# Attention beside a gated MLP on one core: the spatial stage in cycles of eight steps

## The chip, the core and the metric

The kernel runs on one core of a Trainium2 chip. The core has a matrix engine (TensorE, PE in the profile, with its weight loads shown as PEld), a vector engine (VectorE, DVE), an engine for functions of one value (ScalarE, ACT), a general engine (GpSimd, POOL) and one that issues transfers (SyncE, SP). Matrix products land in PSUM, of which the kernel uses eight banks of 128 partitions by 512 numbers; VectorE and ScalarE read them from there. The metric is the device time of one execution in microseconds (us); smaller is better.

## What is computed

One normalised input of 2048 rows and 512 columns feeds two branches, whose outputs are added to the input.

```python
xn = layernorm(x)                         # 2048 x 512
# A: attention, 32 heads of 16
q, k, v = split(xn @ wqkv)
p = softmax(q @ k.T * 16 ** -0.5)         # 32 x 2048 x 2048
a = (p @ v) @ wo
# B: gated MLP with a product over the rows
z = gelu(xn @ w_in)                       # 2048 x 1792
z1, z2 = z[:, :896], layernorm(z[:, 896:])
g = w_sp @ z2 + b_sp[:, None]             # w_sp: 2048 x 2048
b = (z1 * g) @ w_out
out = x + a + b
```

All is in 32-bit numbers. The "dense" products (all but attention's) are made in three parts, high by high, low by high and high by low, from operands split in a high and a low part.

## The kernel before

**Attention as 1024 steps.** Two heads share a pass: half 0 of TensorE's rows holds one, half 1 the other. There are 16 pairs of heads, 4 blocks of 512 queries each and 16 blocks of 128 keys each, so 16 x 4 x 16 = 1024 steps. A step makes, for each of its two heads,

- the scores of 128 keys against 512 queries (`score`, tile `st`, L1274) and their exponentials on ScalarE (L1277, tile `pf`, a buffer of two halves, `PF` = 6 buffers);
- the maxima that a later step needs (`max_one`, tile `mx`, L904): the scores the other way round, and a reduction on VectorE (L905). They run `LEAD` = 26 steps ahead; every 16 steps `max_fin` gathers them and sends them through memory into rows of Q;
- the V products (`pv`, tile `o`, L1232): the exponentials against V and a column of ones, for four column tiles of TensorE at once, added up in one bank over 16 steps.

Scores, maxima and dense products are "lanes": they use 64 rows of TensorE, and two lanes, one on each half, run at the same time. I call two such lanes a pair. The V products use all 128 rows in tiles of 32 columns.

**Cycles.** The loop at the end of `fused_block` goes on by `steps` steps at a time, four of them (`STEPS`). A cycle is: `gather` takes dense products from the front of `queue`; `share` says how many of them go into this cycle; `fill` orders the scores of these steps, the maxima and the dense products on the two halves; `pv_some` issues V products up to step `b + steps - 2`, so they lag by two steps; then the copies of finished accumulators and the gathering of maxima. Every bank of scores or maxima is one of five (`rsum`, tags r0 to r4): a product that comes sixth waits until ScalarE or VectorE has emptied one. Two more banks (d0, d1) hold dense sums, one holds `o`.

**Order.** `fill` plans with its own numbers for time (`SLOT`, `ROUND`, `EXP`, `RED`): it tries greedy orders, then `better` moves products about. `length` and `rollout` price an order by its end and by how far the work left on ScalarE and VectorE goes beyond it (`TURN`).

**Dense work.** `queue` holds six generators: `qk_first`, `z2_all`, `z1_all`, `spatial`, `mlp_out` (mo), `attn_out` (ao). `halves` makes two sums at a time; each half of TensorE adds to one sum, and at each number in `cuts` the halves change sums, with a break in `gather` (`SWAP`). In `spatial` a group is two blocks of 128 columns of z2 against one block of 512 rows of `w_sp`: 16 cells of 3 products, 48 slots, twice, so 192 lanes; each fourth group of a block of rows has one block of columns (`whole`, 96 lanes). Its operands are 16 pieces of weights (`wsp`, split by GpSimd in `prepare`) and pieces of z2 (`zs`, fetched by `load_z`), all from a ring of `RING` = 25 pieces of 4 KB a partition. `pace` and `credit` spread what dense work is left over what steps are left.

Of the kernel before, what the change touches and what calls it, by code (L numbers as in the profile page):

```python
# [33 lines left out]
GC = 0.7978845608028654  # L34
RING = 25
WARM = 15
LEAD = 26
PF = 6
SWAP, END, GATE = 1.25, 1.5, 1.75
STEPS = 4  # L40
# [9 lines left out]
CAP = 3.3  # L50
FIRST = 6
BIAS = 0.0, 0.15, 0.3, 0.6


@with_exitstack
def fused_block(ctx, tc, x, wqkv, wo, w_in, w_spT, b_sp, w_out, out):
# [74 lines left out]
    def slow(us, fn, *args):  # L131
        later(us, waiting.append, (fn, args))
# [10 lines left out]
    def clock():  # L143
        return max(lanes)
# [28 lines left out]
    def later(us, fn, *args):  # L173
        late.append((clock() + us, len(late), fn, args))
# [540 lines left out]


    def spatial():
        zp, z1s, hls = {}, {}, {}
# [25 lines left out]
        for n, (g, fs) in enumerate(groups):  # L744
# [39 lines left out]
            cells = [(lambda s=s: part(s)) for s in range(NT)]  # L784
            want = STEPS * pace + credit / 4
            cuts = (12, 24, 36) if want > 11.4 else (12, 20, 36) if want > 10.2 else (12, 20, 32)
            if single:
# [10 lines left out]
            else:  # L798
                yield from halves(accs, cells, cuts, done)
                for u, f in enumerate(fs):  # L800
# [324 lines left out]
    with tc.manual_schedule(engines=engines):  # L1125
# [90 lines left out]
        maxed = []  # L1216
        lastS = [0, 0]

        def pv(n, a, w):
# [111 lines left out]
        def rollout(ns, want, start, most, bias, extra, flip, rng):  # L1331
# [57 lines left out]
            end_ = max(l)  # L1389
            cost = end_ + 0.3 * sum(max(0.0, v - end_ - TURN) for v in load_) - GAIN * more  # L1390
            return cost, ops

        def length(ops, want, start):
# [29 lines left out]
            end_ = max(l0, l1)  # L1423
            return end_ + 0.3 * (max(0.0, va - end_ - TURN) + max(0.0, vd - end_ - TURN))

# [95 lines left out]
        while b < N or done < N:  # L1521
            steps = 1 if b < 0 else STEPS if b else 2
            ns = [n for n in range(b, b + steps) if 0 <= n < N]
            ms = [m for m in range(b + LEAD, b + LEAD + steps) if m < NSTEP]
            for n in range(b, b + steps):
# [4 lines left out]
                if n > 16 and n % 16 == 2 and n // 16 + 3 < NG * NP:  # L1530
                    load_q(n // 16 + 3)
            pause = max(0, pause - steps)
# [5 lines left out]
            gather(FIRST if b < 0 else 0)  # L1538
            fill(ns, ms, len(slots) if b < 0 else share())
# [3 lines left out]
            if b >= 0:  # L1543
                pv_some(min(b + steps - 2, N))
            nds = []
# [79 lines left out]
```

## Time and profile before

| what | value |
|---|---|
| median of 2 runs | 1791.36 us (1790.3 and 1792.41) |
| the profiled execution | 1790.37 us, its span 1788.3 us |
| granted TensorE clock, mean | 0.999 |
| matmul records | 14419 |
| from the first product of the spatial stage's first cycle | 600.85 us into the span |
| of the first mo cycle | 1467.72 us |
| of the first ao cycle | 1672.52 us |

The span is cut into places by time from its start. A row of the timeline has the start, the length, the engine, the line, the operation, output and inputs by the program's names, the shape, and how many such instructions were merged. A row of the table by stretches has the stretch, its length, and the busy time of PE, PEld, DVE, ACT and POOL with instruction counts, then the granted clock, the share of DMA time and GB/s. The rows themselves stand in the prediction, where they are used. The eight V products that a cycle of four steps issues are 16 records in the trace, four a step.

### The profile page before, as it was taken

How to read it: one execution, taken by the hardware profiler on the slowest of the kernel's cores; microseconds unless marked ns; L12 is line 12 of the kernel's file. 1: busy time of each engine (PE TensorE's matmuls, PEld its weight loads, DVE VectorE, ACT ScalarE, POOL GpSimd, SP SyncE). 2: the span in 40 equal slices, each digit the busy share in tenths (PEclk: the TensorE clock that was granted, in tenths of full speed). 3: DMA queues.
4: the chain of work that ended last, by engine and by line, in shares of the span. 5: the costliest groups of instructions: out<-in, count | busy, mean ns of one | idle time of the engine just before them, and what ended most of it. 6: DMA issues, size and time to landing. Idle time of an engine off the chain costs nothing.

```text
span 1788.3 us, 37962 instructions
## 1 busy us (share of the span) xinstructions
PE 1777.3 (99%) x14419; PEld 1140.7 (64%) x14419; DVE 1449.6 (81%) x2604; ACT 1267.0 (71%) x2351; POOL 782.5 (44%) x815
## 2 busy tenths in 40 slices
PE   9999999999999999999999999999999999999998
PEld 7876666666666666666666566666666666666664
DVE  5288888988888888888888888888877888888872
ACT  5338788887777777777777777777776777677765
POOL 4257676777412542257334573224765261003220
PEclk9999999999999999999999999999999999999999
DMA  7552443534645744356445564345766454454534
GB/s 282 201 171 78 133 127 104 170 88 125 198 150 172 221 140 116 109 171 183 133 144 176 173 195 115 105 126 164 200 180 179 142 169 134 149 170 150 160 108 135
DMA packets 218254, 274.63 MB, mean 154 GB/s; under 512 B 35752, under 2 KB 119352, under 8 KB 216632
## 3 DMA queue, kind: packets, MB, share of 16 engines
q1 hardware_dynamic: 215336, 263.47, 49.1%
q0 software_dynamic: 2592, 8.46, 1.2%
q8 instruction: 114, 1.87, 0.5%
q14 instruction: 68, 0.56, 0.1%
q10 hardware_dynamic: 144, 0.26, 0.0%
HBM read 178.55 MB, written 93.58 MB: 152 GB/s over the span
## 4 chain that ended last, share of the span: by engine, by line
PE 96%; DMA 1%; DVE 1%; ACT 1%; SPq 0%; issue 0%; POOL 0%; DVEq 0%; POOLq 0%; ACTq 0%
PE o L1232 26%; PE st L1274 18%; PE sp L233 17%; PE mx L904 13%; PE z2p L233 5%; PE mo L233 4%; PE z1p L233 3%; PE qk L233 3%; PE ao L233 2%; PE duo L233 2%; PE v L221 1%; PE v L222 1%; PE v L223 1%; DMA zs<-z2scr 0%; PE qk L221 0%; PE qk L222 0%
## 5 line engine op out<-in xcount | busy, mean ns | idle before, releaser
L905 DVE TENSOR_REDUCE mm<-mx 128x1 f32<-128x512 f32 x2048 | 1291.2, 685 | 249.4 <-PE mx L904 214.6
L1277 ACT ACTIVATE pf<-st 128x512 f32<-128x512 f32 x2048 | 1102.9, 601 | 361.9 <-PE mx L904 211.1
L1274 PE MATMUL st<-qst,kst 50*128 50x512 f32 x2048 | 764.4, 410 | 0.8 <-ACT pf L1277 0.7
L904 PE MATMUL mx<-kst,qst 48*128 48x512 f32 x2048 | 752.3, 412 | 0.1
L1274 PEld LDWEIGHTS st<-qst,kst 50*128 50x128 f32 x2048 | 361.0, 185 | 248.1 <-issue 116.8
L233 PE MATMUL sp<-wsp,zs 64*128 64x512 f32 x2688 | 510.2, 393 | 0.0
L1232 PE MATMUL o<-pf,vall 128*32 128x512 f32 x4096 | 492.5, 598 | 0.0
L904 PEld LDWEIGHTS mx<-kst,qst 48*128 48x128 f32 x2048 | 361.8, 185 | 63.4 <-ACT pf L1277 11.6
L233 PEld LDWEIGHTS sp<-wsp,zs 64*128 64x128 f32 x2688 | 366.2, 186 | 29.9
L1232 PEld LDWEIGHTS o<-pf,vall 128*32 128x32 f32 x4096 | 107.0, 109 | 235.2 <-issue 215.7
L233 PE MATMUL mo<-wout,hp 64*128 64x512 f32 x672 | 124.5, 392 | 0.0
L233 PEld LDWEIGHTS mo<-wout,hp 64*128 64x128 f32 x672 | 90.5, 186 | 9.6
L539 POOL TENSOR_TENSOR hhl<-z1i 128x512 f32<-128x512 f32 x28 | 29.2, 1042 | 148.0 <-DMA z1i<-z1scr 118.4
L78 ACT ACTIVATE e<-o 128x512 f32<-128x512 f32 x64 | 38.4, 599 | 70.0 <-PE o L1232 65.8
L861 POOL TENSOR_TENSOR xr<-mox,xr 128x512 f32<-128x512 f32 x8 | 10.3, 1285 | 131.3 <-ACT mox L78 131.3
L545 POOL TENSOR_SCALAR hhl<-hhl 128x512 f32<-128x512 f32 x28 | 17.4, 621 | 104.0 <-ACT hhl L78 104.0
L967 POOL TENSOR_TENSOR ob<-ob 128x512 f32<-128x512 f32 (+1 forms) x16 | 20.7, 1292 | 96.3 <-DMA ob<-rscr 96.3
L805 POOL TENSOR_TENSOR hhl<-hhl,brow 128x512 f32<-128x512 f32 x12 | 15.4, 1287 | 83.5 <-ACT hhl L78 80.7
L233 PE MATMUL ao<-wo,op 64*128 64x512 f32 x288 | 51.9, 392 | 0.0
L586 POOL TENSOR_TENSOR z<-z,z2u 128x896 fp32r<-128x896 f32 x16 | 34.1, 2130 | 27.4 <-ACT z2u L78 27.4
L1039 POOL TENSOR_TENSOR fin<-aox,fin 128x512 f32<-128x512 f32 x8 | 10.3, 1282 | 74.9 <-ACT aox L78 74.9
L233 PEld LDWEIGHTS ao<-wo,op 64*128 64x128 f32 x288 | 36.4, 186 | 4.1
(293 smaller groups left out, 1955.6 us busy)
## 6 DMA issues: line engine op xcount, KB each, us to landing
zs<-z2scr SPq DMA_DIRECT2D x112, 512.0 KB
escr<-e SPq DMA_DIRECT2D x60, 256.0 KB
hscr<-hhl SPq DMA_DIRECT2D x28, 512.0 KB
xscr<-xnT POOLq DMA_DIRECT2D x16, 512.0 KB, 4.9
qscr<-qkhl SPq DMA_DIRECT2D x16, 512.0 KB
kscr<-qkhl SPq DMA_DIRECT2D x16, 512.0 KB
qst<-qscr SPq DMA_DIRECT2D x128, 64.0 KB
hp<-hscr SPq DMA_DIRECT2D x16, 512.0 KB
```

Of the source, the lines that this page charges most:

```text
L78: return nc.scalar.activation(out, in_, func, **kw)
L221: nc.tensor.matmul(acc, lh, rh, start=first, stop=False)
L222: nc.tensor.matmul(acc, ll, rh, start=False, stop=False)
L233: made[half] = lambda: nc.tensor.matmul(acc, prod[0][rows], prod[1][rows], start=start, stop=stop)
L539: gps(0.0022 * n).tensor_mul(u, x, x)
L586: gps(2.1).tensor_sub(low, z, u)
L904: nc.tensor.matmul(acc, qst[c][rows, t * P:(t + 1) * P], kst[p % 2][rows, kc * 512:(kc + 1) * 512], start=True, stop=True)
L905: nc.vector.tensor_reduce(mmax[i // 16][:, j, t, kc:kc + 1], acc, AX.X, ALU.max)
L967: gps(1.3).tensor_mul(both[rows, 0, :], both[rows, 0, :], both[rows, 2, :])
L1232: nc.tensor.matmul(acc[cols:cols + VW, a:a + w], vpack(kt - 1 + r, 2 * p + j), pf[:, j * 512 + a:j * 512 + a + w], start=kt == 1 and a == ...
L1274: nc.tensor.matmul(st, kst[p % 2][rows, kt * P:(kt + 1) * P], qst[c][rows, :], start=True, stop=True)
L1277: nc.scalar.activation(full[n][:, j * 512:(j + 1) * 512], st, AF.Exp, scale=0.25)
```

## The change

The exponentials get eight buffers, the ring 23 pieces: 8 KB a partition move from one to the other. While the spatial stage runs (the list `wide` is not empty), a cycle has eight steps if its first step is a multiple of eight and at least 20 dense slots are gathered, and takes up to 24 of them in one batch; otherwise four steps. `cuts` become (24, 24), so that a batch ends where the halves change sums. In a cycle that ends at a multiple of four, V products are issued up to its last step, with no lag. `gather` now runs before the steps are counted. A piece of z counts as there 4 us after its issue, and one of the second half up to 4 us before that. `slack` replaces `TURN`, for ScalarE and VectorE apart, by the length of the V products to come. Once two generators are left in `queue`, the pace aims at an end of mo at step 926 (`BEGIN`), and a batch may be cut in parts of six slots instead of eight.

```diff
-RING = 25
+RING = 23
-PF = 6
+PF = 8
+BEGIN = 926
...
+                if end_ and f == 6:
+                    wide.append(True)
...
-            later(4.0, zp.update, {(g, f, i): t})
+            zp[g, f, i], due[g, f, i] = t, clock() + 4.0
...
-                if (g, s) not in wsp or any((g, f, s // 4) not in zp for f in fs):
+                if (g, s) not in wsp or any(due.get((g, f, s // 4), 1e9) > clock() + s // 4 % 2 * 4.0 for f in fs):
...
-            want = STEPS * pace + credit / 4
-            cuts = (12, 24, 36) if want > 11.4 else (12, 20, 36) if want > 10.2 else (12, 20, 32)
+            cuts = (24, 24)
...
+        wide.clear()
...
-            cost = end_ + 0.3 * sum(max(0.0, v - end_ - TURN) for v in load_) - GAIN * more
+            cost = end_ + 0.3 * sum(max(0.0, v - end_ - s_) for v, s_ in zip(load_, slack)) - GAIN * more
...
-            n = max(round(r / max(aim + credit / 4, 3)), math.ceil(r / (CAP * STEPS)), 1)
-            n = min(n, max(r // 8, 1))
+            if wide:
+                return 8 if steps == 4 and b % 8 and r >= 20 else math.ceil(r / max(math.ceil(r / (3.4 * steps)), 1))
+            n = max(round(r / max(aim + credit / 4, 3)), math.ceil(r / (CAP * steps)), 1)
+            n = min(n, max(r // (6 if len(queue) < 3 else 8), 1))
...
+            if b > 0:
+                pause = max(0, pause - turned)
+                gather(0)
+                if wide:
+                    if b % 8 == 2:
+                        steps = 6
+                    elif b % 8 == 0 and len(slots) >= 20:
+                        steps = 8
+                elif b % 4 == 0:
+                    steps = 6
+            turned = steps
+            held = 2 if b < 0 or (b + steps) % 4 else 0
+            gone_ = 0.43 * (min(b + steps - held, N) - done) + 0.34
+            slack[:] = gone_ - (0 if held else 0.95), gone_
...
+                if len(queue) == 2:
+                    pace = max((todo - 192) / max(BEGIN - b, 4), 0)
...
-                pv_some(min(b + steps - 2, N))
+                pv_some(min(b + steps - held, N))
```

What this makes of the order is seen on TensorE. First, the end of a cycle in the spatial stage, before. The names are those of the lists above (`st` scores, `mx` maxima, `sp` dense products of this stage, `o` V products from one buffer of exponentials each, `x2` for two rows alike); brackets name the engines or queues whose semaphore a row waits for.

```order
L233 MATMUL sp_2_1_9683<-wsp_3_8390,zs_3_0_9334 128x512
L904 MATMUL mx_1_9849<-kst_90,qst_87 128x512 [waits Activation_49]
L1274 MATMUL st_0_9852<-qst_85,kst_90 128x512 [waits DVE_49]
L1232 MATMUL o_0_9659<-pf_9719,vall 32x512 x2
L1232 MATMUL o_0_9659<-pf_9741,vall 32x512 x2
L1232 MATMUL o_0_9659<-pf_9784,vall 32x512 x2
L1232 MATMUL o_0_9659<-pf_9801,vall 32x512 x2
L1274 MATMUL st_0_9865<-qst_85,kst_90 128x512 [waits Activation_49]
```

The same place after:

```order
L234 MATMUL sp_2_1_9716<-wsp_7_8748,zs_3_1_9682 128x512
L1280 MATMUL st_0_9885<-qst_85,kst_90 128x512 [waits DVE_49]
L1238 MATMUL o_0_9684<-pf_9720,vall 32x512 x2
L1238 MATMUL o_0_9684<-pf_9739,vall 32x512 x2
L1238 MATMUL o_0_9684<-pf_9770,vall 32x512 x2
L1238 MATMUL o_0_9684<-pf_9785,vall 32x512 x2
L1238 MATMUL o_0_9684<-pf_9807,vall 32x512 x2
L1238 MATMUL o_0_9684<-pf_9812,vall 32x512 x2
L1238 MATMUL o_0_9684<-pf_9823,vall 32x512 x2
L1238 MATMUL o_0_9684<-pf_9839,vall 32x512 [waits Activation_49]
L1238 MATMUL o_0_9684<-pf_9839,vall 32x512
L1280 MATMUL st_0_9908<-qst_86,kst_90 128x512 [waits DMAHW2_49]
```

Four buffers of exponentials were used up in one group of V products, and now eight are, the last of them filled in the same cycle, with a wait for ScalarE.

Second, TensorE in the mo stage, before: the end of a cycle that has 24 dense products (`mo`).

```order
L233 MATMUL mo_1_22195<-wout_21147,hp_0_21829 128x512
L904 MATMUL mx_0_22263<-kst_90,qst_88 128x512 [waits DVE_49]
L233 MATMUL mo_1_22195<-wout_21249,hp_0_21829 128x512
L904 MATMUL mx_0_22267<-kst_90,qst_88 128x512 [waits Activation_49]
L233 MATMUL mo_1_22195<-wout_21249,hp_0_21829 128x512
L233 MATMUL mo_0_22194<-wout_21249,hp_0_21827 128x512
L233 MATMUL mo_1_22195<-wout_21249,hp_0_21829 128x512
L1274 MATMUL st_0_22273<-qst_87,kst_90 128x512 [waits DVE_49]
```

After, the end of one that has 12:

```order
L234 MATMUL mo_0_21308<-wout_20444,hp_0_20778 128x512 x2
L234 MATMUL mo_1_21309<-wout_20444,hp_0_20780 128x512 x2
L1280 MATMUL st_0_21364<-qst_88,kst_89 128x512 [waits Activation_49]
L909 MATMUL mx_1_21369<-kst_90,qst_85 128x512 [waits DVE_49]
L909 MATMUL mx_0_21372<-kst_90,qst_85 128x512 [waits Activation_49]
L909 MATMUL mx_1_21375<-kst_90,qst_85 128x512 [waits DVE_49]
L1280 MATMUL st_0_21378<-qst_88,kst_89 128x512 [waits Activation_49]
```

Scores and maxima, each waiting for a bank that another engine empties, now stand together with no dense product between them. In counts: the spatial stage had 137 cycles of four steps and has 45 of eight and 36 of four; mo had 32 cycles of 18 to 24 dense products and has 41, of which 21 have 14 or fewer. Scores, maxima, exponentials, V products and dense products are as many as before.

More of the change, by code (lines that the diff above doesn't have):

```diff
@@ L714, in sp_weights @@
         return f"wsp{g}_{s}", w_spT[s * P:(s + 1) * P, g * 512:(g + 1) * 512], 512
+    wide = []
     def spatial():
-        zp, z1s, hls = {}, {}, {}
+        zp, due, z1s, hls = {}, {}, {}, {}
         def load_z(g, f, i):
@@ L1217, in fused_block @@
         lastS = [0, 0]
+        slack = [TURN, TURN]
         def pv(n, a, w):
@@ L1423, in length @@
             end_ = max(l0, l1)
-            return end_ + 0.3 * (max(0.0, va - end_ - TURN) + max(0.0, vd - end_ - TURN))
+            return end_ + 0.3 * (max(0.0, va - end_ - slack[0]) + max(0.0, vd - end_ - slack[1]))
         def better(cost, ops, want, start, rng, n):
@@ L1531, in fused_block @@
                     load_q(n // 16 + 3)
-            pause = max(0, pause - steps)
+            if b <= 0:
+                pause = max(0, pause - steps)
             if b >= 0:
@@ L1535, in fused_block @@
                 pace = (todo - spare) / max(N - 4 - b, 4)
+                if len(queue) == 2:
+                    pace = max((todo - 192) / max(BEGIN - b, 4), 0)
                 aim = steps * max(pace + 0.5 * (not ms), 0)
                 credit = min(credit + aim, 4 * steps)
-            gather(FIRST if b < 0 else 0)
+            if b <= 0:
+                gather(FIRST if b < 0 else 0)
             fill(ns, ms, len(slots) if b < 0 else share())
```

## The prediction

> **What bounds the kernel now.** I read the page's busy shares and its chain first.
>
> ```profile
> PE 1777.3 (99%) x14419; PEld 1140.7 (64%) x14419; DVE 1449.6 (81%) x2604; ACT 1267.0 (71%) x2351; POOL 782.5 (44%) x815
> ...
> PE 96%; DMA 1%; DVE 1%; ACT 1%; SPq 0%; issue 0%; POOL 0%; DVEq 0%; POOLq 0%; ACTq 0%
> ```
>
> TensorE is never seen idle, and 96% of the chain is its own. But ends of matmuls are modelled, so a full row does not say that every microsecond is needed. What a cycle is worth must be read from its length. I therefore looked at the timeline of TensorE in the stretch where a cycle with 24 dense products (twelve pairs) is followed by one with only 6. A cycle here runs from the first score to the next first score after the V products.
>
> ```profile
> 1304.86 0.50 PE L1274 MATMUL st<-qst,kst 50*128 50x512 f32 x1
> ...
> 1305.66 0.86 PE L233 MATMUL sp<-wsp,zs 64*128 64x512 f32 x6
> ...
> 1309.38 0.39 PE L1274 MATMUL st<-qst,kst 50*128 50x512 f32 x1
> 1309.70 1.92 PE L1232 MATMUL o<-pf,vall 128*32 128x512 f32 x16
> 1311.56 0.50 PE L1274 MATMUL st<-qst,kst 50*128 50x512 f32 x1
> ...
> 1315.78 1.92 PE L1232 MATMUL o<-pf,vall 128*32 128x512 f32 x16
> 1317.64 0.50 PE L1274 MATMUL st<-qst,kst 50*128 50x512 f32 x1
> ```
>
> The full cycle takes 1311.56 - 1304.86 = 6.70 us. The nearly empty one takes 1317.64 - 1311.56 = 6.08 us, though it has nine pairs of products less. So there are two limits. The timelines of VectorE and ScalarE in the same stretch name the second.
>
> ```profile
> 1312.12 4.97 DVE L905 TENSOR_REDUCE mm<-mx 128x1 f32<-128x512 f32 x8 [1.66 <-PE mx L904]
> ...
> 1309.84 0.60 ACT L1277 ACTIVATE pf<-st 128x512 f32<-128x512 f32 x1 [0.32 <-PE st L1274]
> ...
> 1312.24 4.25 ACT L1277 ACTIVATE pf<-st 128x512 f32<-128x512 f32 x8
> ```
>
> In the nearly empty cycle the eight maxima run without a gap for 4.97 us and the eight exponentials for 4.25 us. Sixteen scores and maxima pass through five PSUM banks, and TensorE must wait for a bank. Those three fences are the kernel in small: **a cycle is paid by TensorE if it has enough dense products, and by the emptying of the five banks if it has not.**
>
> The second limit also holds in a run, not only once. The table by stretches gives the spatial stage, the stage of the last product of the gated branch (mo), and eight cycles in a row with 16 dense products.
>
> ```profile
> 600.85:1467.72 866.87, 866.77 (x7076) 539.72 (x7073) 726.19 (x1291) 625.91 (x1173) 399.67 (x408) 1.00 0.53 155
> 1467.72:1672.52 204.80, 204.80 (x1700) 128.26 (x1696) 173.51 (x307) 145.85 (x273) 36.99 (x40) 1.00 0.49 152
> 1001.53:1050.39 48.86, 48.86 (x388) 28.60 (x384) 42.15 (x76) 36.79 (x70) 30.74 (x32) 1.00 0.57 171
> ```
>
> 48.86 / 8 = 6.11 us for a cycle of sixteen pairs (eight of scores and maxima, eight dense). The granted clock is 1.00 in all three, so it is no term of the sum.
>
> **Prices.** The six dense products at 1305.66 are three pairs in 0.86 us, and a lone pair lasts 0.39 in these rows, so a pair costs (0.86 - 0.39) / 2 = 0.235 us. The V products of one step are four records; the weight loads show their spacing.
>
> ```profile
> 1037.02 0.13 PEld L1232 LDWEIGHTS o<-pf,vall 128*32 128x32 f32 x4 [0.30 <-issue]
> 1037.45 0.13 PEld L1232 LDWEIGHTS o<-pf,vall 128*32 128x32 f32 x4 [0.30 <-issue]
> ```
>
> That is 0.43 us a step. A full cycle of four steps has 20 pairs, so what is left over, the entry to and the exit from the V products, is 6.70 - 20 x 0.235 - 4 x 0.43 = 0.28 us; with 0.23 for a pair it is 0.38. I take 0.33. This is what a cycle of double length pays once instead of twice: 2 x 6.70 - 0.33 = 13.07, which I take as 13.08 us.
>
> Five cycles with 20 dense products, and one block of four mo cycles with 24, 22, 20 and 18:
>
> ```profile
> 895.07 0.50 PE L1274 MATMUL st<-qst,kst 50*128 50x512 f32 x1
> ...
> 926.53 0.50 PE L1274 MATMUL st<-qst,kst 50*128 50x512 f32 x1
> ...
> 1467.72 0.50 PE L1274 MATMUL st<-qst,kst 50*128 50x512 f32 x1
> ...
> 1493.28 0.50 PE L1274 MATMUL st<-qst,kst 50*128 50x512 f32 x1
> ```
>
> 31.46 / 5 = 6.29 us, and 25.56 us for the block, which leaves 12.57 for 22 and 18 together: 6.47 and 6.10. From 18 downward I price every cycle at 6.11, the mean of the run above, next to the 6.08 of the cycle with 6.
>
> **The change, part by part.** The built order of TensorE gives the counts; the rows above give the prices.
>
> *Spatial stage.* Before: 137 cycles, 548 steps, 866.9 us. After: 45 cycles of eight steps with 48 dense products, 34 of four steps with 18 or fewer (they stand where the 16 weight pieces of the next group are brought in), two with 24; 504 steps. 45 x 13.08 + 34 x 6.11 + 2 x 6.70 = 588.6 + 207.7 + 13.4 = 809.7 us, which is -57.2.
>
> *Stage mo.* The 44 steps that the spatial stage no longer uses do not vanish: the scores, maxima and exponentials are still 1024 steps. The pace aims at step 926 for the start of the next stage, so the same 672 products of mo spread over 166 steps instead of 128. After: one cycle of six steps, 25 cycles of four with 6 to 18 dense products, and fifteen with 18 to 24. The six-step cycle has 24 scores and maxima in place of 16: the emptying part, 6.08 - 1.86 = 4.22 (from 1311.56 to 1315.78), grows to 6.3, and with the V products it is 8.2. 8.2 + 25 x 6.11 + 4 x (6.47 + 6.29 + 6.10) + 3 x 6.70 = 256.5 us against 204.8: +51.7. **Here the gain is given back**: cycles which had up to 24 dense products, and were paid by TensorE, get 12 to 14 and are paid by the banks.
>
> *Ends.* The last cycle of the z1 stage has six steps, takes V products of eight, and has 24 pairs: 24 x 0.235 + 8 x 0.43 + 0.33 = 9.4 for 6.70, +2.7. The end of the program has one full cycle more (+6.70), while the last one, which was filled with 24 dense products, keeps only four scores:
>
> ```profile
> 1772.85 0.73 PE L1274 MATMUL st<-qst,kst 50*128 50x512 f32 x3
> ...
> 1776.29 1.92 PE L1232 MATMUL o<-pf,vall 128*32 128x512 f32 x16
> 1778.14 1.12 PE L1063 MATMUL al<-fin,ident 128*128 128x512 f32 x2
> ```
>
> It took 5.29 us. Bare, it must wait for its four exponentials: 0.68 until the first begins (1311.56 to 1312.24), 2.2 for four, then the second half of the V products, 0.97: 3.9. So +6.70 - 1.4 = +5.3.
>
> *Wait for the own exponentials.* In the spatial stage the V products no longer lag by two steps. The last exponential of the full cycle ends at 1309.84 + 0.60 = 1310.44, 0.74 after the V products begin. In a cycle of four steps its V products come 0.86 after the beginning, in a doubled one 2.58. I take nothing; the cover is the earlier V products, and without it each exponential left over costs 4.25 / 8 = 0.53. Below zero it cannot go: a wait removed here was not seen.
>
> *Buffers.* Eight buffers of exponentials instead of six remove no wait, since none of the eight exponentials above waits between its neighbours. The ring of 23 must hold 16 weight pieces and 6 of z, one spare. Loads of z then stand behind a read of TensorE more often (66 of 112 in the built order, 24 before):
>
> ```profile
> SPq L123 <- PE sp L233: 65.1, 24, 11.1
> ```
>
> Behind such a load stand SP's other transfers: rows of maxima, K, Q. Nothing of TensorE waited for them; a piece is now fetched half a doubled cycle (6.5 us) before its use. I take nothing; if that cover goes, a late piece stalls TensorE by its own lateness. The slack numbers, the due times of z and the limit on a batch's parts change only the order, priced above.
>
> **Sum.** -57.2 + 51.7 + 2.7 + 5.3 = +2.5 us on the profiled execution of 1790.4 (span 1788.3, and 2.1 around it), so 1792.9; the median of the runs, 1791.4, is 1.0 above it. I write 1793.
>
> The Trainium skill, page "TensorEngine Tiling (Array Packing)", section "PSUM Bottleneck", warns that packing speeds up TensorE but not the emptying of PSUM, which may become the limit. That speaks against this change, for it saves TensorE's time alone. The trace agrees (6.08 us for the nearly empty cycle). With the rule the sum is 1793; without it, with every cycle priced by pairs, it would be the first rival's 1757.
>
> **Rivals.**
> 1. *The floor gives way*, and sparse cycles cost only their pairs (2.0 + 0.235 a pair: 5.76 with 16 dense products, 5.53 with 14, 5.29 with 12, 4.59 with 6). That takes 19 us off the spatial stage and 17 off mo: 1757. For it: VectorE is busy for 42.15 of the 48.86 us, so it is not full itself. Against: 6.08 and 48.86 / 8.
> 2. *Slower: the V products wait for exponentials of their own cycle.* With two left over when the V products begin, each of the 34 short cycles pays 0.74 + 0.53 - 0.86 = 0.41: +14, 1807. It turns into a slowdown of 2% (36 us more) if the doubled cycles too wait 0.45, which needs four to five exponentials left at their end: 34 x 0.45 + 45 x 0.45 = 36, so 1829. Against: the order puts one score at the end of the doubled cycle.
> 3. *Doubling saves nothing*: the left-over 0.33 goes with the number of V rounds and not with the entry. 45 x 0.32 = +14: 1807. Against: the spacing of 0.43 is even within a group.
> 4. *Late pieces of z or of weights*, one microsecond at each of some 16 groups: +16, 1809. The DMA share in the spatial stage, 0.53, leaves room.
>
> **How the numbers follow.** Chances: my sum 0.70, the rivals 0.05, 0.12, 0.07, 0.06. The sum's own bounds: a doubled cycle from 13.02 to 13.40 (-3, +14), a sparse cycle from 5.98 (the shortest, 1044.41 to 1050.39, below) to 6.31 in the 34 of the spatial stage (-8, +7).
>
> ```profile
> 1044.41 0.50 PE L1274 MATMUL st<-qst,kst 50*128 50x512 f32 x1
> ...
> 1050.39 0.50 PE L1274 MATMUL st<-qst,kst 50*128 50x512 f32 x1
> ```
>
> So 1782 to 1804 for my case, and 1780 to 1812 with rivals 3, 4 and the milder form of 2. Two per cent, 1755 to 1827, is about what a measurement of this kernel can tell from no change: faster 0.02 (the far end of rival 1), same 0.95, slower 0.03 (the full form of rival 2).
>
> **What would show it.** Right: some 81 groups of V products in the spatial stage, doubled cycles near 13.1, the stage near 810 us, mo near 256 with cycles of 6.1 whatever their dense products. Wrong: sparse cycles near 5.5 (rival 1), weight loads of the V products that wait for an exponential (2), doubled cycles at 13.4 (3), TensorE behind a DMA of z (4).

## The result, and the profile after

The changed kernel takes 1805.80 us (two runs, 1803.64 and 1807.95) against 1791.36 us before: a ratio of 1.0083, with a 95% interval of 1.0067 to 1.0099. It is slower by 0.8%, which is less than the two per cent that the chances went by. The forecast was 1793, with a range of 1780 to 1812.

The page's busy shares and chain of waits after:

```profile
PE 1784.3 (99%) x14419; PEld 1167.2 (65%) x14419; DVE 1450.8 (81%) x2604; ACT 1250.6 (69%) x2351; POOL 781.0 (43%) x815
...
PE 96%; DMA 1%; DVE 1%; ACT 1%; POOL 0%; issue 0%; SPq 0%; DVEq 0%; ACTq 0%; POOLq 0%
```

Nothing in these two lines tells that the kernel is another one. TensorE is "99% busy" in both, and the chain is 96% its own in both. The table by stretches tells more. It has the spatial stage, mo, and ao with its last V products (length, busy time of PE, PEld, DVE, ACT and POOL with their records, granted clock, DMA share, GB/s):

```profile
609.98:1421.03 811.05, 810.79 (x6724) 533.84 (x6720) 674.26 (x1192) 564.94 (x1084) 393.06 (x402) 1.00 0.54 161
1421.03:1681.11 260.08, 256.93 (x1997) 153.30 (x1993) 219.66 (x392) 185.40 (x350) 39.55 (x44) 0.99 0.43 128
1681.11:1791.52 110.41, 110.41 (x944) 67.65 (x940) 68.69 (x123) 76.61 (x145) 22.88 (x22) 1.00 0.43 133
```

With the cycles counted in the timeline of TensorE (from the first score after one group of V products to the first score after the next), both profiled executions come apart into these stages. The span grew by 13.5 us, from 1788.3 to 1801.8.

| stage | before, us | after, us | forecast | measured |
|---|---|---|---|---|
| prologue, to the end of the first V products | 134.8 | 140.5 | 0 | +5.75 |
| z2, Q and K | 302.8 | 302.8 | 0 | 0 |
| z1 | 161.7 | 165.1 | +2.7 | +3.4 |
| spatial stage | 866.9 | 811.05 | -57.2 | -55.8 |
| mo | 204.8 | 260.1 | +51.7 | +55.3 |
| ao, to the last V products | 105.6 | 110.4 | +5.3 | +4.8 |
| rest | | | 0 | +0.1 |

The spatial stage did what it was to do. These are two of its doubled cycles in the timeline of TensorE:

```profile
646.77 0.50 PE L1280 MATMUL st<-qst,kst 50*128 50x512 f32 x1
...
656.26 3.64 PE L1238 MATMUL o<-pf,vall 128*32 128x512 f32 x32
659.83 0.50 PE L1280 MATMUL st<-qst,kst 50*128 50x512 f32 x1
...
669.38 3.64 PE L1238 MATMUL o<-pf,vall 128*32 128x512 f32 x32
672.95 0.49 PE L1280 MATMUL st<-qst,kst 50*128 50x512 f32 x1
```

659.83 - 646.77 = 13.06 and 672.95 - 659.83 = 13.12 us; the 45 of them lie between 13.06 and 13.25, mean 13.10. The V products of eight steps take 3.57 us in each, twice the 1.86 of four steps less 0.15. Sparse cycles, a little earlier, with 16 and 14 dense products:

```profile
616.24 0.50 PE L1280 MATMUL st<-qst,kst 50*128 50x512 f32 x1
...
622.36 0.50 PE L1280 MATMUL st<-qst,kst 50*128 50x512 f32 x1
...
628.41 0.49 PE L1280 MATMUL st<-qst,kst 50*128 50x512 f32 x1
```

6.12 and 6.05 us. In mo the 21 cycles with 14 or fewer take 6.05 us on average.

What the forecast lacked happened in the prologue. There TensorE multiplies Q, K and z1 (`duo`), and in the rows GpSimd (POOL) splits weight pieces into high and low parts (`w`), and takes the low parts of Q and K (`qkhl`):

```profile
106.14 0.56 POOL L328 CAST w<-w_1r 128x448 fp32r<-128x448 f32 x1 [12.66 <-PE duo L234]
...
107.88 3.80 POOL L493 TENSOR_TENSOR qkhl<-duo,qkhl 128x512 fp32r<-128x512 f32 x3
...
114.25 0.63 ACT L79 ACTIVATE qkhl<-duo 128x512 fp32r<-128x512 f32 x1 [13.56 <-DMA qscr<-qkhl]
...
115.42 1.91 PE L234 MATMUL duo<-xnT,wqk 64*128 64x512 f32 x9 [3.42 <-ACT duo L79]
```

Read from the top: GpSimd stood 12.66 us before a weight piece, because TensorE still read the block of the ring into which it was to go. The three low parts of Q and K stood behind it in GpSimd's queue. Their stores were late, so ScalarE waited 13.56 us for a store of Q, and TensorE 3.42 us for ScalarE. The table by stretches over that place shows a second cost behind the first:

```profile
108.00:110.00 2.00, 2.00 (x20) 1.49 (x18) 1.41 (x3) 0.00 (x0) 2.00 (x2) 1.00 0.00 0
...
112.00:114.00 2.00, 0.00 (x0) 0.00 (x0) 1.44 (x4) 0.00 (x0) 0.00 (x0) 1.00 1.03 381
...
117.00:119.00 2.00, 2.00 (x12) 1.52 (x12) 0.75 (x2) 0.00 (x0) 0.00 (x0) 0.50 0.81 300
119.00:121.00 2.00, 2.00 (x16) 1.59 (x14) 0.72 (x2) 0.00 (x0) 0.00 (x0) 0.72 1.03 292
```

```profile
116.00:122.00 6.00, 6.00 (x40) 4.76 (x40) 2.48 (x4) 0.85 (x2) 0.22 (x1) 0.72 0.77 251
```

After the idle time the granted clock fell to 0.50. TensorE is shown as busy all the time there, but with 12 products in 2 us where it had 20 before the wait. In the kernel before, ScalarE waited 0.7 us for a store of Q, and the same place has neither the gap nor the slow clock:

```profile
112.00:116.00 4.00, 3.90 (x34) 3.12 (x32) 3.30 (x6) 0.29 (x1) 1.84 (x3) 1.00 0.77 215
116.00:122.00 6.00, 6.00 (x54) 4.55 (x52) 4.59 (x8) 0.58 (x2) 3.31 (x4) 1.00 0.48 132
```

An idle time with a slow clock behind it stands at the start of mo too, in the cycle of six steps, timeline first:

```profile
1421.04 0.49 PE L1280 MATMUL st<-qst,kst 50*128 50x512 f32 x1
...
1423.29 0.46 PE L234 MATMUL mo<-wout,hp 64*128 64x512 f32 x1 [1.51 <-POOL wout L329]
...
1432.14 0.50 PE L1280 MATMUL st<-qst,kst 50*128 50x512 f32 x1
```

```profile
1421.00:1423.30 2.30, 0.79 (x9) 0.34 (x5) 0.69 (x1) 1.08 (x2) 2.22 (x4) 1.00 1.00 371
1423.30:1427.30 4.00, 4.00 (x21) 3.81 (x23) 2.67 (x4) 2.11 (x4) 3.76 (x5) 0.59 0.77 267
```

TensorE waited 1.51 us for GpSimd's split of a `wout` piece, and then ran 4 us at a mean clock of 0.59. The cycle took 1432.14 - 1421.04 = 11.10 us.

### The profile page after: what moved, and what is told of

Its sections match the earlier page's. It is cut to its first block, busy times and chain, and to the rows that moved or that the text cites. A ratio compares the mean times of both kernels' runs of the same rounds, so it can differ in the third digit from the quotient of the medians.

```text
span 1801.8 us, 38004 instructions
## 1 busy us (share of the span) xinstructions
PE 1784.3 (99%) x14419; PEld 1167.2 (65%) x14419; DVE 1450.8 (81%) x2604; ACT 1250.6 (69%) x2351; POOL 781.0 (43%) x815
## 4 chain that ended last, share of the span: by engine, by line
PE 96%; DMA 1%; DVE 1%; ACT 1%; POOL 0%; issue 0%; SPq 0%; DVEq 0%; ACTq 0%; POOLq 0%
PE o L1238 26%; PE sp L234 18%; PE st L1280 17%; PE mx L909 12%; PE z2p L234 5%; PE mo L234 5%; PE z1p L234 4%; PE qk L234 3%; PE ao L234 2%; PE duo L234 2%; PE v L222 1%; PE v L223 1%; PE v L224 1%; DMA z1scr<-z 0%; DVE mm L910 0%; PE qk L222 0%
## 5 line engine op out<-in xcount | busy, mean ns | idle before, releaser
L1283 ACT ACTIVATE pf<-st 128x512 f32<-128x512 f32 x2048 | 1086.8, 604 | 334.8 <-PE mx L909 182.2
L1238 PE MATMUL o<-pf,vall 128*32 128x512 f32 x4096 | 485.9, 597 | 0.0
L1238 PEld LDWEIGHTS o<-pf,vall 128*32 128x32 f32 x4096 | 115.0, 109 | 247.6 <-issue 216.4
L234 PE MATMUL mo<-wout,hp 64*128 64x512 f32 x672 | 138.9, 401 | 1.5 <-POOL wout L329 1.5
L866 POOL TENSOR_TENSOR xr<-mox,xr 128x512 f32<-128x512 f32 x8 | 10.3, 1285 | 182.6 <-ACT mox L79 178.8
L963 POOL TENSOR_TENSOR os<-os 128x32 f32<-128x32 f32 (+1 forms) x16 | 4.0, 251 | 83.0 <-DMA os<-escr 59.0
```

The costliest lines, as they stand in the source:

```text
L234: made[half] = lambda: nc.tensor.matmul(acc, prod[0][rows], prod[1][rows], start=start, stop=stop)
L1238: nc.tensor.matmul(acc[cols:cols + VW, a:a + w], vpack(kt - 1 + r, 2 * p + j), pf[:, j * 512 + a:j * 512 + a + w], start=kt == 1 and a == ...
L1283: nc.scalar.activation(full[n][:, j * 512:(j + 1) * 512], st, AF.Exp, scale=0.25)
```

## Experiments

Three theories were to be told apart. The first: the smaller ring costs the prologue, by the queue of GpSimd. The second: the doubled cycle saves TensorE 0.33 us, and this is given back because a cycle has a floor, set by the emptying of the PSUM banks, which more cycles now reach. The rival to both: the doubling saves nothing, or the loss comes from the new pacing. Ratios are to the kernel before, run on the same chip.

| kernel | us | ratio (95% interval) |
|---|---|---|
| before with a ring of 23 | 1794.06 | 1.0022 (1.0014 to 1.0031) |
| before with ring 23 and eight buffers | 1795.77 | 1.0032 (1.0020 to 1.0045) |
| the same, three blocks counted as free | 1789.53 | 0.9996 (0.9987 to 1.0005) |
| changed, three blocks counted as free | 1800.93 | 1.0054 (1.0042 to 1.0067) |
| changed, no doubled cycles | 1811.86 | 1.0114 (1.0098 to 1.0129) |
| changed, doubled cycles with 40 dense products | 1811.58 | 1.0115 (1.0101 to 1.0128) |
| the same, three blocks counted as free | 1806.47 | 1.0093 (1.0076 to 1.0110) |
| changed, no pace for mo | 1812.90 | 1.0122 (1.0107 to 1.0137) |
| changed, half of each maximum | 1797.72 | 1.0041 (1.0028 to 1.0054) |
| changed, half of each exponential | 1797.63 | 1.0040 (1.0026 to 1.0054) |
| changed, both halved | 1773.77 | 0.9909 (0.9892 to 0.9926) |
| before, both halved | 1767.88 | 0.9876 (0.9861 to 0.9891) |

### The ring alone

```diff
-RING = 25
+RING = 23
```

> The kernel before with the ring of 23 blocks in place of 25, and nothing else; its cycles stay what they were. Theory A (the smaller ring alone delays the prologue, because a weight piece then waits for a block that TensorE still reads, and GpSimd's split of Q and K stands behind that piece): the first V products come about 5.7 us later, ScalarE's split of Q and K waits some 13 us for a store, and the time is about 1797 us, +5.8. Rival B (the delay in the prologue comes from the new cycles or the eight buffers of exponentials): the prologue is unchanged and the time is 1791 us. Rival C (the ring also starves the spatial stage of pieces of z): 1805 us, with TensorE behind transfers of z there.

It became 1794.06 us, 0.22% above the kernel before, between A and B. Where the time went is as A said. The waits up to 150 us (what waited, for what, us in total, times, the longest) have the same pair, and the later stages are as before:

```profile
ACT qkhl L78 <- DMA qscr<-qkhl: 12.3, 1, 12.3
POOL w L327 <- PE duo L233: 12.1, 1, 12.1
```

```profile
604.35:1471.02 866.67, 866.33 (x7076) 536.77 (x7072) 725.78 (x1291) 625.79 (x1173) 398.43 (x407) 1.00 0.52 155
1471.02:1675.67 204.65, 204.65 (x1700) 127.86 (x1696) 173.41 (x307) 145.86 (x273) 36.93 (x40) 1.00 0.48 152
```

The first V products end 4.1 us later than before (138.84 for 134.78 in the table's sense). TensorE's wait for ScalarE is 2.2 us here, and the clock behind it (0.87 over the 4 us from 112, 0.80 over the next 6) costs 4 x 0.13 + 6 x 0.20 = 1.7 us more, which together are 3.9. C falls: the ring starves nothing in the spatial stage, 866.67 for 866.87.

### Ring and buffers without the new cycles

```diff
-RING = 25
+RING = 23
-PF = 6
+PF = 8
```

> The kernel before with the ring of 23 and with eight buffers of exponentials, and nothing else; its cycles hold what they held. The ring alone cost 3.9 us, all of it in the prologue, where the changed kernel loses some 6. Theory A (the two buffer numbers make up the whole loss of the prologue): 1796 to 1798 us, with the first V products 6 us later than before and later stages unchanged. Rival B (eight buffers neither cost nor gain, and the other 2 us of the prologue come from the rest of the change): 1794 to 1795 us. Rival C (eight buffers remove waits in the later stages): below 1793 us.

1795.77 us, and 4.7 us more in the prologue of the profile (139.45); spatial stage and mo are as before (867.4 and 204.7). By the time, +0.32% or 5.5 us (3.6 to 8.1 by its interval), A and B cannot be told apart with certainty; A is nearer. C falls: eight buffers remove no wait that mattered.

```diff
-        freed = [clock()] * 4
+        freed = [clock()] * 3
```

This line stands in the prologue (`qk_first`). It says how many blocks of the ring the planner may count as free for weights of z2 at that moment. Added to the kernel above:

> The same kernel, with three blocks of the ring counted as free in the prologue in place of four (24 dense products of the z2 stage move from the prologue into a cycle of their own). Theory A (GpSimd's wait for a block of the ring, ahead of its part of Q and K, is the whole cost of the smaller ring): ScalarE's wait for the store of Q goes and the time is 1790 to 1793 us, that of the kernel before. Rival B (the smaller ring costs in another way, or the moved products cost as much as the wait): 1794 to 1798 us.

A holds, half a microsecond below its range: 1789.53 us, 0.9996 of before. The waits and the clock of this kernel:

```profile
POOL w L327 <- PE duo L233: 3.0, 1, 3.0
ACT qkhl L78 <- DMA qscr<-qkhl: 0.7, 1, 0.7
```

```profile
112.00:116.00 4.00, 3.89 (x34) 3.11 (x32) 3.28 (x6) 0.55 (x2) 2.36 (x4) 1.00 0.80 223
116.00:122.00 6.00, 6.00 (x55) 4.54 (x54) 4.55 (x8) 0.26 (x1) 2.93 (x4) 1.00 0.36 115
```

ScalarE's wait fell from 12.2 us to 0.7, TensorE has 34 and 55 products at a clock of 1.00 where the changed kernel's rows had a long gap and a slow clock, and the first V products end 4.1 us earlier than without this line (135.4 for 139.45). So the smaller ring need not bring the wait: a count of four free blocks, which did no such harm with 25, let GpSimd come to a piece too early. That the wait is the whole price is not shown. The line also changes the plan behind it: z2, Q and K take 309.8 us for 302.8, and the spatial stage has 135 cycles for 137 and takes 854.7 us for 867.4. The count of three with a ring of 25 was not run, so a part of the 0.36% may belong to this other plan.

### The same line in the changed kernel

> The changed kernel, in which the prologue counts three blocks of the ring as free for weights of the z2 stage in place of four, so that GpSimd does not come to a piece whose block TensorE still reads. Theory A (GpSimd's wait in the prologue is what costs the 5.75 us there): ScalarE's wait of 13.6 us for a store of Q goes, the first V products come some 5 us earlier, and the time is about 1800 us. Rival B (the wait hides behind other work and the delay comes from something else): 1806 us with the first V products as late as in the changed kernel.

1800.93 us, A by its time. This and the run before it agree on what the line is worth: 1.0083 - 1.0054 = 0.29%, and 1.0032 - 0.9996 = 0.36%, 5 to 6.5 us, each give or take some 3 us by the intervals. The 0.54% that are left, 9.7 us, belong to the rest of the change. In the profile the spatial stage has 809.7 and mo 258.1 us, about what the changed kernel has. ScalarE's long wait is gone there, but the first V products end 3.0 us earlier (137.6 for 140.5) and not 5: the granted clock was 0.74 over the 20 us from 130, which is 5.2 us lost. The moved products make z2, Q and K longer by 7.7 us and z1 shorter by 4.1, so mo begins only 0.6 us earlier. By its stages, then, this run does not single out the price of the wait.

### No doubled cycles

```diff
-                    elif b % 8 == 0 and len(slots) >= 20:
-                        steps = 8
```

> The changed kernel without cycles of eight steps: the spatial stage is again in cycles of four steps, 123 of them with 492 steps, 89 of which have 24 dense products; all else (maxima, exponentials, buffers, ring, pacing) stays. Theory A (a doubled cycle saves one entry to and one exit from the V products, 0.3 us): some 44 more entries at 0.30 to 0.35 us, +14 us, 1819 us; a pair of cycles of four steps takes 13.4 us where a doubled one takes 13.1. Rival B (the doubling itself saves nothing, since the left-over goes with each round of V products): 1806 us.

1811.86 us: 0.31% above the changed kernel, 5.6 us with intervals that barely overlap, which neither theory gave. The price of a cycle is A's: the 89 cycles with 24 dense products take 6.72 us each, so two take 13.44 where a doubled one takes 13.10. That is 0.34 for each of 45, 15.3 us. But the planner built another mix:

```profile
611.24:1418.77 807.53, 807.39 (x6629) 518.60 (x6625) 648.41 (x1162) 572.20 (x1058) 390.78 (x400) 1.00 0.54 160
1418.77:1686.88 268.11, 268.06 (x2062) 157.78 (x2058) 228.94 (x415) 195.03 (x368) 40.73 (x44) 1.00 0.43 129
```

Its spatial stage needs 492 steps in place of 504, since the 34 sparse cycles hold 72 more dense products, and is shorter (807.5 for 811.05); mo has 8 steps more and takes 268.1. So the doubling is worth 0.34 us a cycle, as the forecast had it, and rival B falls by the lengths of the cycles; what it is worth in the sum depends on where the steps go.

### Dense products spread over more steps

```diff
-            cuts = (24, 24)
+            cuts = (20, 20, 40, 40)
```

> The changed kernel with the dense products of a group of the spatial stage cut into 20, 20, 40 and 40 parts in place of 24 and 24 and the rest: a doubled cycle has 40 dense products in place of 48, the spatial stage takes 568 steps in place of 504, and stage mo has 130 steps with 18 to 26 dense products in a cycle in place of 170 with 6 to 24. The total of scores, maxima, V products and dense products is the same. Theory A (the saving was given back because cycles with 18 dense products or fewer are paid by the emptying of the PSUM banks, and putting dense products evenly over the steps avoids such cycles): about 1788 us, range 1780 to 1795. Rival B (steps and dense products cost the same wherever they stand, and the loss has other causes): 1803 to 1808 us.

Both missed: 1811.58 us. The plan did what was meant, mo fell to 207.9 us, but two prices were wrong. First, a doubled cycle with fewer dense products does not get shorter by their pairs. Here is one, in TensorE's timeline, between two groups of V products:

```profile
698.50 0.50 PE L1280 MATMUL st<-qst,kst 50*128 50x512 f32 x1
...
707.79 3.19 PE L1238 MATMUL o<-pf,vall 128*32 128x512 f32 x28
710.91 0.50 PE L1280 MATMUL st<-qst,kst 50*128 50x512 f32 x1
```

12.41 us. The 43 of them take 12.38 to 12.97, mean 12.59, which is twice the 6.30 of a single cycle with 20: at 40 dense products nothing is saved. TensorE's own price would be 13.10 less four pairs, 13.10 - 4 x 0.235 = 12.16, so each lies 0.43 above it, some 18 us in all; what holds it there was not tried. Second, the steps ran out before the dense products did, and the last 144 of these stood alone at the end:

```profile
1503.86:1711.74 207.88, 207.88 (x1724) 130.39 (x1721) 174.62 (x313) 149.21 (x277) 51.36 (x57) 1.00 0.48 152
...
1775.38:1810.40 35.02, 25.68 (x196) 18.50 (x192) 7.09 (x11) 4.51 (x12) 4.55 (x4) 0.94 0.36 121
```

35.02 us after the last V products, where the changed kernel has 10.3: 24.7 us for 72 pairs, 0.34 a pair and not 0.235, with TensorE busy for 25.68 of the 35.02.

With the three blocks in addition:

> The changed kernel with both edits: doubled cycles of 40 dense products (cuts of 20, 20, 40 and 40) and three blocks counted as free in the prologue. If the spread and the prologue are separate costs, their gains add: the time of the spread alone less about 5 us, 1780 to 1786 us, below both kernels. Rival (the prologue's delay is absorbed later, since the steps that are late there find slack elsewhere): the same time as the spread alone.

1806.47 us. The two ratios differ by 0.22%, 3.9 us, so the prologue's gain adds, as far as two intervals that overlap a little can tell; the level was as wrong as that of the spread.

### No pace for mo

```diff
-                if len(queue) == 2:
-                    pace = max((todo - 192) / max(BEGIN - b, 4), 0)
```

> The changed kernel without the pace that aims at step 926 for the end of stage mo: mo has 186 steps in 46 cycles and the next stage, ao, about 12. Theory A (steps are conserved: what the spatial stage leaves undone is paid at 6.1 us for four steps wherever it stands): 1803 to 1809 us, with mo longer by some 20 us and ao shorter by as much. Rival B (the pace itself makes mo slow): 1790 us or less, with ao no longer than in the changed kernel.

1812.90 us, above A's range by 4 and far from B:

```profile
1419.54:1703.34 283.80, 283.19 (x2156) 163.77 (x2153) 243.40 (x439) 205.85 (x391) 47.43 (x52) 1.00 0.39 122
1703.34:1782.76 79.42, 77.71 (x681) 47.60 (x678) 39.28 (x70) 53.21 (x102) 12.01 (x12) 1.00 0.51 153
1782.76:1810.20 27.44, 19.17 (x144) 12.85 (x140) 6.40 (x10) 3.56 (x9) 3.26 (x3) 0.90 0.21 77
```

mo is longer by 23.7 us and ao shorter by 31.0: steps are conserved. The 96 dense products that ao no longer covers with steps stand alone at the end (27.44 us for 10.3), 0.36 us for a pair, as in the spread. That is the part which A left out.

### What sets the floor

Three kernels halve what VectorE and ScalarE do with a bank, and leave TensorE's instructions as they are. The first takes each maximum over half of the columns:

```diff
-        nc.vector.tensor_reduce(mmax[i // 16][:, j, t, kc:kc + 1], acc, AX.X, ALU.max)
+        nc.vector.tensor_reduce(mmax[i // 16][:, j, t, kc:kc + 1], acc[:, :256], AX.X, ALU.max)
```

> The changed kernel in which VectorE takes each maximum over 256 of the 512 keys of a bank only; the products, their order and all else stay. Theory A (the floor of the sparse cycles is the emptying of the banks, and VectorE's part of it sets it): cycles with 18 dense products or fewer fall from 6.05 us to between 5.3 and 5.8, full cycles stay at 6.70 and doubled ones at 13.1, and the time falls by 10 to 30 us to 1776 to 1796 us. Rival B (ScalarE's exponentials or TensorE's own products set the floor): the sparse cycles stay at 6.0 to 6.1 and the time at 1803 to 1806 us.

Against A: cycles with 12 and 14 dense products in mo fall only from 6.05 to 5.97 us, and those with 16 in the spatial stage stay at 6.10 (6.12 before the edit). The time, which fits neither theory's range, fell by more than these explain (0.42%). Of the 5.9 us by which the two spans differ, 5.1 lie in mo, and 3.5 of these in four cycles: the one of six steps took 9.46 for 11.10, and the three with 24 dense products 6.78 for 7.41 on average.

The second takes each exponential over half of the columns:

```diff
-            nc.scalar.activation(full[n][:, j * 512:(j + 1) * 512], st, AF.Exp, scale=0.25)
+            nc.scalar.activation(full[n][:, j * 256:(j + 1) * 256], st[:, :256], AF.Exp, scale=0.25)
...
+        def half_of(pf, j, w):
+            h = pf[:, j * 256:(j + 1) * 256]
+            return h if w == 256 else h.unsqueeze(1).to_broadcast([P, 2, 256])
...
-                    nc.tensor.matmul(acc[cols:cols + VW, a:a + w], vpack(kt - 1 + r, 2 * p + j), pf[:, j * 512 + a:j * 512 + a + w], start=kt == 1 and a == 0, stop=kt == NT - 1 and a + w == 512)
+                    nc.tensor.matmul(acc[cols:cols + VW, a:a + w], vpack(kt - 1 + r, 2 * p + j), half_of(pf, j, w), start=kt == 1 and a == 0, stop=kt == NT - 1 and a + w == 512)
```

`half_of` hands the same 256 columns to a V product twice, so the other half of the exponentials is left out and the V products stay as long as they were.

> The changed kernel in which ScalarE takes each exponential over 256 of the 512 queries of a bank only, and the V products read these 256 twice, so that their count, length and order stay; the maxima are whole. With halved maxima alone the sparse cycles fell only from 6.05 to 5.97 us. Theory A (the emptying of the banks sets the floor, and either of the two engines is slow enough to set it by itself): the sparse cycles stay between 5.9 and 6.1 us and the time between 1797 and 1806 us. Rival B (the exponentials alone set the floor): cycles of 12 to 16 dense products fall to 5.3 to 5.8 us, and the time by 15 to 30 us.

A: the sparse cycles of up to 16 dense products are at 5.99 to 6.05 us, the time at 1797.63. Neither engine alone makes the floor. Both edits together:

> The changed kernel with both halved, maxima and exponentials, over 256 of 512 columns; products, their count and their order stay. Theory A (emptying sets the floor): the sparse cycles fall to TensorE's count, 2.05 us and 0.235 for each pair: 5.8 us with 16 dense products, 5.6 with 14, 5.3 with 12, 4.6 to 5 with 6; doubled cycles of 48 stay at 13.1; the time is 1770 to 1785 us. Rival B (the floor is TensorE's own: its order, or the entry to the V products): sparse cycles stay above 5.9 and the time at 1797 us or more.

A, for the most part: 1773.77 us. These are the same two cycles with 16 and 14 dense products as in the section on the result:

```profile
611.01 0.49 PE L1284 MATMUL st<-qst,kst 50*128 50x512 f32 x1
...
616.81 0.49 PE L1284 MATMUL st<-qst,kst 50*128 50x512 f32 x1
...
622.47 0.49 PE L1284 MATMUL st<-qst,kst 50*128 50x512 f32 x1
```

5.80 and 5.66 us, for 6.12 and 6.05. With 16 dense products that is TensorE's own count, 16 x 0.235 + 4 x 0.43 + 0.33 = 5.81. Doubled cycles stay at 13.10. But cycles with 12 take 5.63 (mo) and 5.69 (spatial stage) on average, and those with 6 take 5.43 and 5.49, where the count gives 5.34 and 4.64: a second floor lies near 5.5 us. What sets that one wasn't tried.

The partner, the kernel before with the same two edits:

> The kernel before with both halved in the same way, as the partner of the changed kernel with both halved. Theory A (the doubling saves 0.33 us on each of 45 cycles, and the change gave this back because it made more cycles sparse): before gains little from a lower floor, since its cycles have 16 dense products or more: 1778 to 1786 us; and the changed kernel with both halved is faster than this one by 2 to 8 us, where with the floor in place it was slower by 14. Rival B (the change loses for reasons that have nothing to do with the floor): the changed kernel stays slower by about 14 us here too.

Neither: it gains 1.24% and is at 1767.88 us, so the changed kernel is behind it by 5.9 us. The stages of both, the changed one first:

```profile
605.00:1404.02 799.02, 798.80 (x6724) 529.26 (x6721) 435.76 (x1192) 401.44 (x1084) 393.79 (x402) 1.00 0.54 164
1404.02:1653.76 249.74, 247.26 (x1998) 152.77 (x1994) 145.25 (x392) 126.59 (x350) 39.71 (x44) 0.99 0.44 132
```

```profile
595.31:1448.13 852.82, 852.13 (x7076) 525.14 (x7073) 475.28 (x1290) 435.74 (x1173) 399.25 (x408) 1.00 0.52 157
1448.13:1651.74 203.61, 203.61 (x1700) 126.56 (x1696) 114.12 (x306) 100.92 (x273) 37.29 (x40) 1.00 0.48 153
```

The changed kernel now pays +46.1 in mo where it paid +55.3, and still saves 53.8 in the spatial stage. With z1 (+3.3), ao (+4.1) and nothing else this sums to -0.3; the whole difference that is left is the prologue, 139.7 against 133.3, +6.4. With the floor in place the same four stages summed to +7.6. So with the banks emptied sooner the change stands some 8 us better against its partner. Of these 2.7 are the six-step cycle (8.40 for 11.10), whose extra was not the floor alone: in the section on the result it waits for `wout`. The expectation had forgotten the prologue, and had taken the cycles with 12 and 14 all the way down to their count.

## Why the prediction was right, and where it was wrong

**Right: the limit, and the two prices.** A doubled cycle was priced at 13.08 us and took 13.10; a sparse one at 6.11 and took 6.00 to 6.28 in the spatial stage (6.12 on average) and 6.05 in mo with 14 dense products or fewer. The spatial stage came out at 811.05 for 809.7. The run without doubled cycles shows the 0.34 us that an entry and exit cost, by another way than the forecast found it (0.33).

**Right: the gain is given back in mo.** It was shown, not only summed: without the pace the steps go from ao to mo, one for one; and with the emptying of the banks halved on both engines, mo's extra falls from 55.3 to 46.1, 2.7 of it in the six-step cycle. The section "PSUM Bottleneck" of the Trainium skill's page "TensorEngine Tiling (Array Packing)", which says that faster use of TensorE may leave the emptying of PSUM as the limit, agrees with these runs, with one thing added by them: two engines share the emptying here, and relief for one alone moves a sparse cycle by some 0.1 us.

**Wrong: the ring of 23, for which the forecast says "I take nothing".** This is the step that failed: +5.75 us in the prologue of the profile, 3.9 us in the time with the ring alone, 5 to 6.5 us by the pairs of runs. The forecast looked for the cost of the ring where the change is, at the loads of z in the spatial stage and at what stands behind them in SP's queue. There it found a cover, and the cover held: TensorE has no wait in the list for the whole spatial stage, and SP's queue waited 139 us for TensorE there, no more than the 157 us before. But the ring is shared with the prologue, and there GpSimd's queue had the low parts of Q and K behind a weight piece. The sentence on the buffers should have asked for every stage that takes blocks from the ring. The granted clock, "no term of the sum" because the rows that were read had 1.00, was one behind this wait, where it took 1.7 us, and at the start of mo, where it took 1.6.

**Mis-sized: the six-step cycle of mo**, 8.2 forecast and 11.10 measured. mo now begins 47 us earlier in the program (1421.04 for 1467.72), and its first product met a `wout` piece that GpSimd had only just split. The forecast had counted its scores and maxima, and not asked whether its operands were there. In four other profiles with this cycle (in two of them one engine empties its banks sooner) it took 9.30 to 9.72, so over a microsecond is usual and the rest this execution's; with both engines relieved it took 8.40. A further 2.1 us are in mo's three cycles with 24 dense products, one of which holds a wait of 1.6 us for a load of Q; its 25 cycles with 6 to 18 dense products gave 1.4 back (6.06 on average for 6.11). The last z1 cycle, six steps as well, took 10.66 for 9.4, and the one that it replaces had taken 7.36, not 6.70.

**The sum.** 5.75 in the prologue, 3.6 in mo, 1.4 in the spatial stage and 0.7 in z1, less 0.5 at the end: 11 us, which is what lies between the forecast's +2.5 and the 13.5 of the span.

**What was luck.** The median of 1805.80 lies above 1804, where the forecast ended its own case (the profiled execution, 1803.64, is just below), and within 1812 only by the room left for rivals that did not come. The bounds of that case were also added up wrongly: +14 and +7 above 1793 are 1814. Neither was reached, since doubled cycles stayed at 13.10 and sparse ones at 6.12; what filled the room were the prologue and the six-step cycles. And two per cent is not what a measurement can tell from no change: the interval here, from two runs, is 0.3% wide.

**The rivals.** The first, that the floor gives way, fell with the cycles at 6.05. The second, V products waiting for exponentials of their own cycle: in the doubled cycles the V products take 3.57 us throughout; in some sparse ones 1.93 to 2.01 in place of 1.85, a tenth of a microsecond. The third, that doubling saves nothing, fell by the cycles of 6.72. It is true at 40 dense products, where the doubled cycle takes 12.59, twice 6.30. The fourth, late pieces: none in the spatial stage; the one that came late was `wout`.

**Why there was little to win.** The spatial stage and mo together have 3360 dense products over 670 to 676 steps, 20 for four steps. At 20 a cycle takes 6.30, and TensorE's count, 18 x 0.235 + 4 x 0.43 + 0.33, is 6.28: the kernel before stood close to where the two limits meet. A cycle that takes more dense products than that leaves fewer for another, which then pays the floor. 45 x 0.34 = 15.3 us were saved at the one side, and the 21 cycles of mo at 14 or fewer, those with 6 to 14 in the spatial stage and the ends cost it again. This is a sum by counts; the runs show the 0.34, the floor, and some 8 us of what the floor costs. No version tried that does all the work is faster than the kernel before; the nearest (0.9996) is that kernel itself with the smaller ring made harmless.

What stays open: whether the eight buffers add a part of their own to the prologue (5.5 us with them, 3.9 without, intervals that overlap; TensorE's wait for ScalarE is 2.2 us in both profiles), why that wait is 3.42 us in the changed kernel, and what holds sparse cycles at 5.5 us once both engines are relieved.

## What to carry to other kernels

When a change makes TensorE's share cheaper in one stage, work out for the whole program how much dense work is left per step, and price the steps that it sets free at the floor of the stage that will get them. When a shared buffer gets smaller, look at every stage that draws from it, and at what stands behind its users in their queues, not only at the stage that is changed. If a long wait appears in a stage that the change doesn't touch, look for a count in the planner that was right for the old size.

## What the runs showed of the hardware

A short idle time of TensorE can cost more than its length. In the prologue 3.42 us without a product were followed by a clock of 0.50 over 2 us and 0.72 over the next 2; over the 6 us from 116 the mean was 0.72, a loss of 6 x 0.28 = 1.7 us. With the ring alone 2.2 us were followed by a loss of 1.7 us as well. At the start of mo 1.51 us were enough, and cost 4 x 0.41 = 1.6 us more. But the length alone does not decide. Some 200 us later in the same execution TensorE waited 1.63 us for a load of Q, and the clock stayed at 1.00:

```profile
1630.27 0.47 PE L1280 MATMUL st<-qst,kst 50*128 50x512 f32 x1 [1.63 <-DMA qst<-mscr]
```

```profile
1626.00:1638.00 12.00, 10.37 (x86) 6.40 (x84) 7.86 (x15) 7.34 (x14) 4.41 (x4) 1.00 0.61 174
```

With three blocks counted as free, the changed kernel lost 5.2 us to a slow clock from 130 us on, with no wait of TensorE above 0.5 us just ahead of it. What else decides, the runs do not show. The Trainium skill, page "TensorE: Matmul & The Clock Gate", in its part on the clock gate, says that the clock falls to half after an idle window of about 3.4 us, and that it takes about 3.4 us of work to come back. The half and the time to come back agree (0.50 in one stretch; 1.6 to 1.7 us lost are 3.3 to 3.4 us at half); the first gap agrees too, but gaps of 2.2 and 1.51 us brought the fall as well. Such a stretch is not seen as idle: the row of busy time is full, and only the granted clock, or the count of products in the stretch, tells.
